# Operands of the second token pair split in place, block order of the last first-layer units, and a later start of the second-layer weight conversion

## The chip, the cores and the metric

The kernel runs on one core of a Trainium2 chip, as one launch. The metric is the device time of one execution in microseconds (us); lower is better. The time before is 1125.38 us, the median of three runs (1124.12 to 1126.78).

## What is computed

```python
def reference(q, k, v, tau, moe_*, moe2_*):
    qn, kn = q / (norm(q, axis=1) + 1e-6), k / (norm(k, axis=1) + 1e-6)   # over 6016 tokens
    a = softmax(kn.T @ qn / tau)                                         # 256 x 256
    x = v @ a                                                            # 6016 x 256
    x = (silu(x @ w_gate) * (x @ w_val)) @ w_out                         # d_ff 1536
    h = x @ w_in                                                         # d_ff 2048
    return (h * clip(h + 3, 0, 6) / 6) @ w_out2
```

All weights arrive as 64-bit floats and are rebuilt on the chip into 32-bit ones. Every product is made of 32-bit values split into a high and a low half (high by a ScalarE copy into the reduced format, low by a VectorE subtraction), and three matmuls: high x high, low x high, high x low.

## The kernel before

The 6016 tokens are cut into six pairs of token blocks: five of 2 x 512 tokens and one of 2 x 448. Channel attention comes first; its 256 x 256 matrix is then folded into the two input weights of the first network (`fold`, L601), so that the first network works on v itself.

**The first pair** (token blocks 0 and 1 of pair 0) is done plainly, while the folded weights are still being made: 24 units `(f, b)` of the loop at L926, f over 12 tiles of hidden channels and b over the two blocks. A unit is 12 matmuls into two PSUM banks, SiLU on ScalarE (L951), a product on VectorE (L952), the split of the result (`plain_split`, L918), and a lagging `back()` (L841) of 6 matmuls with `wo`. Banks go round by `next_bank` (b0, b1, a, d); folds take one, units two.

**All later pairs** use a Strassen-like scheme of seven products (`Cube`, L683): a cube handles one tile i of channels (two for the second network) and both blocks of a pair with products p1 to p7, each of three matmuls, into banks a, b0 or b1, and d. p1 writes bank a, p5 bank d, p6 and p4 and p7 a b bank. Layer 1 has 12 cubes for each of pairs 1 to 5, numbered c = 0 to 59 in the loop at L983; layer 2 follows. A cube also issues two `back()`s of an earlier cube.

**Operands.** For a pair, `prep(u)` (L329) takes the raw tokens, forms the differences that the scheme needs and splits seven operands j = 0 to 6. In the kernel before, most are split into a staging place, stored to DRAM (`opd`, L349), and loaded again into one of nine places op0 to op8 (`load_op`, L398) when the pair before has left it. Pair u's operand j lives in op((7u+j) mod 9). For pair 1 operands 0, 1 and 4 are split directly into their places; 2, 3, 5 and 6 go by DRAM, and `arrive` (L907) issues their four loads in the last two units (L972). The nine steps s1 to s9 of `prep(1)` are put on `todo` at unit 18 and issued by `work(3)` from unit 19 on (L956). During the first pair the op places also hold v (`v_hi`, L472: op0, op3 for block 0, op1, op4 for block 1), and work space of the folds (`FA`: op7, op2; `FS`: op8, op5, L598).

**Second-layer weights.** 16 jobs are rebuilt and split by `convert()` (L252) on VectorE, ScalarE and GpSimd, stored to DRAM (L209, L213, L217) and loaded from there when layer 2 nears (`next_weights`, L878). One call of `convert` advances a clock by one; a job has six steps and a new job starts every three, so the whole takes 51 calls and its pattern repeats every six. In steps of that pattern counted from 0: at 2 one store (L209) and a raw load, at 4 and 1 most ScalarE work, at 5 two stores (L213, and L217, which waits for further ScalarE and GpSimd work) and a raw load (L109). It is called in units 19 to 23 and once per cube from c = 0 (L1023), so call number c + 5 falls in cube c.

**Queues.** Every DMA is issued by SP, in program order, and SP waits there for what the DMA needs. The schedule is written by hand: the order of issue in the program is the order on each engine. At the end of a pair, `back()` copies the finished block from PSUM into tile `xo` (L865) and stores it (`x_d`, L869). `xo` and the raw tokens of the next `prep` (`vr`, L302) share one single buffer, so the load of `vr`, issued in the second cube of a pair, waits for those stores; in the third cube the first step of `prep` on ScalarE (L340) waits for the load.

Of the kernel before, what the change touches and what calls it, by code (L numbers as in the profile page):

```python
# [8 lines left out]
F32 = mybir.dt.float32  # L9
F32R = mybir.dt.float32r  # L10
# [8 lines left out]
def channel_attention_then_two_ffns(  # L19
# [24 lines left out]
    nc = tc.nc  # L44
    P = 128
    NTOK, C = q.shape
    NT = NTOK // P
    CT = C // P
# [128 lines left out]
    def sums(S, a11, a12, a21, a22, engine):  # L177

        engine.tensor_tensor(out=S[:, 0], in0=a21, in1=a22, op=ALU.add)
        engine.tensor_tensor(out=S[:, 1], in0=S[:, 0], in1=a11, op=ALU.subtract)  # L180
        engine.tensor_tensor(out=S[:, 2], in0=a11, in1=a21, op=ALU.subtract)
        engine.tensor_tensor(out=S[:, 3], in0=a12, in1=S[:, 1], op=ALU.subtract)
# [69 lines left out]
    def convert():  # L252

        t = clock[0]
        clock[0] += 1
        for j, steps in enumerate(second):
            if 0 <= t - SPAN * j < len(steps):
                steps[t - SPAN * j]()

    def converted():  # L260
        return clock[0] >= SPAN * (len(second) - 1) + len(second[0])


    passed = [0] * 4

    def load_jobs(ahead=RAW):
        while passed[0] < min(len(jobs), passed[1] + ahead):
            jobs[passed[0]].load()
            passed[0] += 1

# [27 lines left out]
    def op_tile(u, j):  # L298
        ops[u, j] = op_p.tile([P, 2, TB], F32R, tag=f"op{(NQ * u + j) % NS}", name="op")
        return ops[u, j]  # L300
# [19 lines left out]
    def stage(u):  # L320

        i = places_st[0] = places_st[0] + 1
        if u == 0 and i % 3 == 0:
            return op_p.tile([P, 2, TB], F32R, tag="op6", name="sp")
        if 0 < u < NP or u >= NP and i % 4 < 2:
            return op_p.tile([P, 2, TB], F32R, tag=f"op{(NQ * (u + 1) + i % 2) % NS}", name="sp")
        return st_p.tile([P, 2, TB], F32R, tag="st", name="st")

    def prep(u, direct=()):  # L329

        n = pairs[u % NP][1]
        x = load_v(u) if u < NP else load_x2(u - NP)
        b11, b21, b12, b22 = x[:, 0, 0, :n], x[:, 0, 1, :n], x[:, 1, 0, :n], x[:, 1, 1, :n]
        opd[u] = dram.tile([P, NQ, 2, TB], F32, tag=f"opd{u}", name="opd")
        of = {0: b11, 1: b11, 2: b22, 3: b21, 4: b22, 5: b12, 6: b21}
        t = {}

        def hi(j):
            t[j] = op_tile(u, j) if j in direct else stage(u - 1)
            nc.scalar.activation(t[j][:, 0, :n], of[j], AF.Copy)  # L340

        def lo(j):
            nc.vector.tensor_tensor(
                out=t[j][:, 1, :n], in0=of[j], in1=t[j][:, 0, :n].bitcast(F32), op=ALU.subtract
            )
            if j in direct:
                return
            stored.add((u, j))
            nc.sync.dma_start(out=opd[u][:, j, :, :n], in_=t[j][:, :, :n].bitcast(F32))  # L349

        def diff(out, a, b):
            nc.vector.tensor_tensor(out=out, in0=a, in1=b, op=ALU.subtract)

        def s1():
            hi(0)

        def s2():
            hi(4)
            lo(0)
            diff(b11, b12, b11)  # L360

        def s3():
            hi(1)
            lo(4)
            diff(b12, b22, b12)

        def s4():
            hi(5)
            lo(1)
            diff(b22, b22, b11)  # L370

        def s5():
            hi(2)
            lo(5)

        def s6():
            hi(3)
            lo(2)

        def s7():  # L380
            lo(3)
            diff(b21, b21, b22)

        def s8():
            hi(6)

        def s9():
            lo(6)

        return [s1, s2, s3, s4, s5, s6, s7, s8, s9]  # L390

    todo = []

    def work(n):
        for _ in range(min(n, len(todo))):
            todo.pop(0)()
# [8 lines left out]
    with tc.manual_schedule():  # L405

        with tc.tile_pool(name="sm", bufs=1) as sm, tc.tile_pool(name="qk", bufs=AHEAD) as qk_p, tc.tile_pool(
# [63 lines left out]

            def v_hi(b):  # L472
                for k in range(CT):
                    t = v0[b, k] = op_p.tile([P, 2, TB], F32R, tag=f"op{b + 3 * k}", name="v0")
                    nc.scalar.activation(t[:, 0], vraw[:, b, k], AF.Copy)

            def v_lo(b):
# [118 lines left out]
            w_in[1, g] = w1_p.tile([P, 2, 2, NQ, P], F32R, tag=f"w{g}", name="w1")  # L596

        FA = [op_p.tile([P, 2 * CT, CW], F32, tag=f"op{i}", name="FA") for i in (7, 2)]  # L598
        FS = [op_p.tile([P, 2 * CT, CW], F32, tag=f"op{i}", name="FS") for i in (8, 5)]

        def fold(m, g):  # L601

# [37 lines left out]
        def w1_hi(g, o, src):  # L640
            hi = w_in[1, g][:, :, 0, o : o + src.shape[1]]
            nc.scalar.activation(hi, src.rearrange("p o (c f) -> p c o f", c=2), AF.Copy)

        def w1_lo(g, o, src):
            hi, lo = (w_in[1, g][:, :, part, o : o + src.shape[1]] for part in range(2))
            src = src.rearrange("p o (c f) -> p c o f", c=2)
            nc.vector.tensor_tensor(out=lo, in0=src, in1=hi.bitcast(F32), op=ALU.subtract)

        def w1_sums(g):
            fa = FA[g % 2]  # L650
            return lambda: sums(FS[g % 2], fa[:, 0], fa[:, 1], fa[:, 3], fa[:, 2], nc.vector)

        def w1_rest(g):
            fs = FS[g % 2]
            return [lambda: w1_hi(g, S1, fs), lambda: w1_lo(g, S1, fs)]

        turn = [0]

        def next_bank(shape):
            tag = ("b0", "b1", "a", "d")[turn[0] % 4]  # L660
# [216 lines left out]

        def next_weights(g):  # L878

            assert converted()  # L880
            if g < NF2 // CT // 2:
                w_in[2, g] = w1_p.tile([P, 2, 2, NQ, P], F32R, tag=f"w{g}", name="w2i")
                nc.sync.dma_start(out=w_in[2, g].bitcast(F32), in_=wi_d[:, 2 * g : 2 * g + 2])
            else:
                last = g >= NG1
                f0 = (g - NF2 // CT // 2) * per_w2
                nf = min(per_w2, NF2 - f0)
                pool, tag = (const, "wo") if last else (w1_p, f"w{g}")
                t = pool.tile([P, NF1 if last else per_w2, 2, C], F32R, tag=tag, name="w2o")
                w_back[g] = (t, f0, nf)  # L890
                nc.sync.dma_start(out=t[:, :nf].bitcast(F32), in_=w2_d[:, f0 : f0 + nf])
# [19 lines left out]
                load_op(u, j, n)  # L911

        units = [(f, b) for f in range(NF1) for b in range(2)]
        LAG = 3
        n = pairs[0][1]
        h_of, last = None, None
# [9 lines left out]
        for i, (f, b) in enumerate(units):  # L926
            w = w_in[1, f // 2][:, f % 2]
            pss = []
            for row in ((A11, A12), (S1, A22)):
                ps = next_bank([P, TB])  # L930
                for k in range(CT):
                    x = v0[b, k]
                    mm3(
                        ps[:, :n],
                        (w[:, 0, row[k], :], w[:, 1, row[k], :]),
                        (x[:, 0, :n], x[:, 1, :n]),
                        k == 0,
                        k == CT - 1,
                    )
                pss.append(ps)  # L940

            def between():
                pump()
                for go in lows:
                    go()
                lows.clear()

            if h_of:
                plain_split(between)
            h = h_tile(1)  # L950
            nc.scalar.activation(h[:, :n], pss[0][:, :n], AF.Silu)  # L951
            nc.vector.tensor_tensor(out=h[:, :n], in0=h[:, :n], in1=pss[1][:, :n], op=ALU.mult)  # L952
            h_of = (f, b, h)
            if i % 4 == 0 and i:
                todo[:0] = w1_rest(i // 4 - 1)
            work(3 if i > 18 else 1)  # L956
            if i > 18 and passed[3] == NJ1:
                convert()
            if i == 10:
                steps1 = prep(1, (0, 1, 4))  # L960
            g = i // 4 + 1
            if i % 4 in (1, 2) and g < NG1:
                m = i % 4 - 1
                need(m, g)
                for go in lows:
                    go()
                lows = [fold(m, g)]
                if m:
                    todo.append(w1_sums(g))
                    if g == NG1 - 1:  # L970
                        todo.extend(steps1)
            if i >= len(units) - 2:  # L972
                for j in ((2, 5), (3, 6))[i - len(units) + 2]:
                    arrive(1, pairs[1][1], j)
            while len(backs) > LAG - 1:
                back()
        plain_split(lambda: None)
        todo[:0] = w1_rest(NG1 - 1)

        prev = None
        for c, key in enumerate(cubes):  # L983
# [36 lines left out]
            cube.after_p3(prev)  # L1020
            if layer == 2:
                work(i > 1)
            elif not converted():  # L1023
                convert()
            if backs:
                back()
# [46 lines left out]
```

## Time and profile before

| | before |
|---|---|
| median of three runs | 1125.38 us (1124.12 to 1126.78) |
| profiled execution, its own time | 1128.53 us |
| its span | 1126.7 us |
| TensorE busy | 1100.6 us, 98% of the span |
| VectorE, ScalarE, GpSimd busy | 797.7, 765.5, 81.4 us |
| mean granted TensorE clock | 0.992 of full |

The span lies 1.83 us below the time of the same execution; the sums are made in that execution. Matmuls are pipelined, so that the busy time of one (some 385 ns) is longer than the distance from start to start, and lost time is read from the starts. The trace names TensorE PE, its weight loads PEld, VectorE DVE, ScalarE ACT, GpSimd POOL, and the DMA issue of SP SPq.

### The profile page before, as it was taken

The page shows a single profiled execution, that of the slowest core. Times are in us where ns is not written, and L with a number is a line of the kernel's source. Part 1 is how long each engine was busy: PE and PEld are TensorE (multiplying, and loading weights), DVE is VectorE, ACT ScalarE, POOL GpSimd, SP SyncE. Part 2 cuts the span into 40 slices and gives each one's busy share as a digit, 9 for nine tenths or more (in the row PEclk, how much of TensorE's full clock was granted, in tenths as well). Part 3 has the DMA queues.
Part 4 walks back from the last instruction along what each step waited for, and adds up shares of the span by engine and source line. Part 5 has one row for each costly group of instructions (what it writes and reads, how often), then busy time and mean ns, then how long its engine had stood idle before and what let it go on. Part 6 is the DMA issues. An engine that isn't in the chain of part 4 may idle for free.

```text
span 1126.7 us, 13789 instructions
## 1 busy us (share of the span) xinstructions
PE 1100.6 (98%) x4896; PEld 922.0 (82%) x4896; DVE 797.7 (71%) x1254; ACT 765.5 (68%) x1329; POOL 81.4 (7%) x92
## 2 busy tenths in 40 slices
PE   8889998999999999999999999999999999999998
PEld 7768886888788788878899888888888888888897
DVE  6869966687687587677566577677677677676665
ACT  6666755676766676666566677767777777777766
POOL 0000002222131122211000000000000000000000
PEclk9899999999999999999999999999999999999999
DMA  9613405434434623622455722522513413324100
GB/s 336 233 56 94 150 19 182 168 127 165 168 145 141 229 94 138 238 91 113 150 214 220 299 107 98 168 90 99 182 57 124 157 75 136 121 78 134 56 1 33
DMA packets 58053, 154.51 MB, mean 137 GB/s; under 512 B 5248, under 2 KB 18048, under 8 KB 56576
## 3 DMA queue, kind: packets, MB, share of 16 engines
q1 hardware_dynamic: 57984, 153.64, 38.3%
q8 instruction: 38, 0.62, 0.2%
q14 instruction: 31, 0.25, 0.1%
HBM read 91.88 MB, written 61.73 MB: 136 GB/s over the span
## 4 chain that ended last, share of the span: by engine, by line
PE 85%; DMA 7%; DVE 4%; ACT 2%; issue 1%; SPq 0%; DVEq 0%; ACTq 0%
PE o L96 37%; PE ps_b L96 20%; PE ps_a L96 13%; PE ps_d L96 13%; DMA x_d<-xo 2%; DMA vr<-in_vT 1%; DMA op<-opd 1%; DVE acc L535 1%; DMA tk<-in_k 1%; PE ps_b L609 1%; DMA tq<-in_q 1%; DMA raw<-in_moe_w_val 1%; DVE m L131 0%; PE warm L435 0%; DVE h L952 0%
## 5 line engine op out<-in xcount | busy, mean ns | idle before, releaser
L778 DVE TENSOR_TENSOR hl<-h,hl 128x512 fp32r<-128x512 f32 (+1 forms) x312 | 209.9, 685 | 158.9 <-ACT hl L712 152.7
L96 PE MATMUL o<-hl,w2o 128*128 128x512 f32 (+1 forms) x1152 | 287.6, 385 | 0.0
L96 PEld LDWEIGHTS o<-hl,w2o 128*128 128x128 f32 x1152 | 215.9, 188 | 40.8 <-DVE hl L778 0.6
L712 ACT ACTIVATE hl<-h 128x512 fp32r<-128x512 f32 (+1 forms) x312 | 187.7, 617 | 73.3 <-DVE h L762 52.7
L96 PE MATMUL o<-hl,wo 128*128 128x512 f32 (+1 forms) x864 | 218.4, 388 | 3.0 <-DVE wo L159 1.6
L96 PEld LDWEIGHTS o<-hl,wo 128*128 128x128 f32 x864 | 162.3, 188 | 34.7 <-DVE wo L159 2.0
L96 PE MATMUL ps_b<-op,w 128*128 128x512 f32 (+1 forms) x540 | 140.0, 385 | 4.7 <-ACT h L712 3.9
L96 PEld LDWEIGHTS ps_b<-op,w 128*128 128x128 f32 x540 | 101.0, 188 | 25.0 <-ACT h L712 5.6
L716 DVE TENSOR_TENSOR h<-h,ps_d 128x512 f32<-128x512 f32 (+1 forms) x108 | 72.5, 671 | 62.5 <-PE ps_d L96 45.7
L96 PE MATMUL ps_b<-op,w2i 128*128 128x512 f32 (+1 forms) x432 | 112.0, 385 | 0.0
L96 PE MATMUL ps_a<-op,w 128*128 128x512 f32 (+1 forms) x360 | 100.3, 387 | 2.5 <-DMA op<-opd 1.5
L96 PE MATMUL ps_d<-op,w 128*128 128x512 f32 (+1 forms) x360 | 100.1, 387 | 1.4 <-DVE h L952 1.4
L712 ACT ACTIVATE h<-ps_b 128x512 f32<-128x512 f32 (+1 forms) x108 | 63.3, 586 | 53.4 <-PE ps_b L96 52.1
L712 ACT ACTIVATE ps_b<-ps_a 128x512 f32<-128x512 f32 (+1 forms) x108 | 61.9, 573 | 51.4 <-PE ps_a L96 51.2
L96 PEld LDWEIGHTS ps_b<-op,w2i 128*128 128x128 f32 x432 | 81.1, 188 | 15.1
L756 ACT ACTIVATE h<-h,three 128x512 f32<-128x512 f32 (+1 forms) x96 | 68.8, 716 | 34.1 <-DVE h L716 32.5
L716 DVE TENSOR_TENSOR h<-h,ps_b 128x512 f32<-128x512 f32 (+1 forms) x108 | 72.4, 671 | 13.1 <-PE ps_b L96 11.8
L96 PEld LDWEIGHTS ps_a<-op,w 128*128 128x128 f32 x360 | 67.8, 189 | 15.6 <-DMA op<-opd 2.0
L96 PE MATMUL ps_d<-op,w2i 128*128 128x512 f32 (+1 forms) x288 | 79.8, 385 | 0.2 <-DMA op<-opd 0.2
L96 PE MATMUL ps_a<-op,w2i 128*128 128x512 f32 (+1 forms) x288 | 79.8, 385 | 0.0
L96 PEld LDWEIGHTS ps_d<-op,w 128*128 128x128 f32 x360 | 67.9, 189 | 14.3 <-DVE h L952 1.9
L762 DVE SCALAR_TENSOR_TENSOR h<-h 128x512 f32<-128x512 f32 (+1 forms) x96 | 65.0, 677 | 12.5 <-ACT h L756 12.5
(132 smaller groups left out, 1320.8 us busy)
## 6 DMA issues: line engine op xcount, KB each, us to landing
op<-opd SPq DMA_DIRECT2D x60, 512.0 KB, 5.1
opd<-sp SPq DMA_DIRECT2D x44, 512.0 KB, 2.7
opd<-st SPq DMA_DIRECT2D x16, 512.0 KB, 2.6
raw<-in_moe_w_out SPq DMA_DIRECT2D x14, 512.0 KB, 4.2
w2i<-wi_d SPq DMA_DIRECT2D x4, 1792.0 KB, 8.1
op<-opd SPq DMA_DIRECT2D x14, 448.0 KB, 4.1
vr<-in_vT SPq DMA_DIRECT2D x10, 512.0 KB, 4.7
x_d<-xo SPq DMA_DIRECT2D x20, 256.0 KB, 5.3
```

The lines of the kernel that those rows point to most:

```text
L96: nc.tensor.matmul(out, lhsT=w, rhs=x, start=first, stop=last, skip_group_check=True)
L535: nc.vector.tensor_tensor(out=acc[:, :n], in0=acc[:, :n], in1=sq[:, :n], op=ALU.add)
L609: nc.tensor.matmul(ps[:, c, :], lhsT=et[:, d, c * P : (c + 1) * P], rhs=w[:, d, :], start=c == 0 and d == 0, stop=d == CT - 1, skip_group_ ...
L712: nc.scalar.activation(out[:, : self.n], src[:, : self.n], AF.Copy)
L716: nc.vector.tensor_tensor(out=out[:, :n], in0=a[:, :n], in1=b[:, :n], op=ALU.add)
L756: nc.scalar.activation(r[:, : self.n], x[:, : self.n], AF.Relu, bias=three)
L762: nc.vector.scalar_tensor_tensor(out=r[:, :n], in0=r[:, :n], scalar=6.0, in1=x[:, :n], op0=ALU.min, op1=ALU.mult)
L778: nc.vector.tensor_tensor(out=hl[:, 1, :n], in0=h[:, :n], in1=hl[:, 0, :n].bitcast(F32), op=ALU.subtract)
```

## The change

The second pair's seven operands are all split directly into their op places: `prep(1)` has six steps d1 to d6 of its own, and the four stores and four loads are gone. For that, block 1 of v moves to op5 and op6, `FS` for odd groups to op1 and for the last group into a raw-weight buffer, and the last four units go block by block: (10,0), (11,0), (10,1), (11,1). `next_bank` starts two banks later. The second-layer jobs are loaded only from cube c = 1, and `convert` is called from cube c = 3 on instead of from unit 19, so call number c - 3 falls in cube c. `next_weights` asserts only the jobs it needs.

```diff
--- before.py
+++ after.py
@@ -257,14 +257,15 @@
             if 0 <= t - SPAN * j < len(steps):
                 steps[t - SPAN * j]()
 
-    def converted():
-        return clock[0] >= SPAN * (len(second) - 1) + len(second[0])
+    def converted(j=-1):
+        return clock[0] >= SPAN * (j % len(second)) + len(second[0])
 
 
     passed = [0] * 4
+    limit = [NJ1]
 
     def load_jobs(ahead=RAW):
-        while passed[0] < min(len(jobs), passed[1] + ahead):
+        while passed[0] < min(limit[0], passed[1] + ahead):
             jobs[passed[0]].load()
             passed[0] += 1
 
@@ -320,13 +321,11 @@
     def stage(u):
 
         i = places_st[0] = places_st[0] + 1
-        if u == 0 and i % 3 == 0:
-            return op_p.tile([P, 2, TB], F32R, tag="op6", name="sp")
         if 0 < u < NP or u >= NP and i % 4 < 2:
             return op_p.tile([P, 2, TB], F32R, tag=f"op{(NQ * (u + 1) + i % 2) % NS}", name="sp")
         return st_p.tile([P, 2, TB], F32R, tag="st", name="st")
 
-    def prep(u, direct=()):
+    def prep(u):
 
         n = pairs[u % NP][1]
         x = load_v(u) if u < NP else load_x2(u - NP)
@@ -336,14 +335,14 @@
         t = {}
 
         def hi(j):
-            t[j] = op_tile(u, j) if j in direct else stage(u - 1)
+            t[j] = op_tile(u, j) if u == 1 else stage(u - 1)
             nc.scalar.activation(t[j][:, 0, :n], of[j], AF.Copy)
 
         def lo(j):
             nc.vector.tensor_tensor(
                 out=t[j][:, 1, :n], in0=of[j], in1=t[j][:, 0, :n].bitcast(F32), op=ALU.subtract
             )
-            if j in direct:
+            if u == 1:
                 return
             stored.add((u, j))
             nc.sync.dma_start(out=opd[u][:, j, :, :n], in_=t[j][:, :, :n].bitcast(F32))
@@ -387,6 +386,39 @@
         def s9():
             lo(6)
 
+        if u == 1:
+
+            def d1():
+                hi(0)
+                hi(3)
+                lo(0)
+
+            def d2():
+                hi(4)
+                lo(3)
+                diff(b11, b12, b11)
+
+            def d3():
+                lo(4)
+                diff(b12, b22, b12)
+                diff(b22, b22, b11)
+
+            def d4():
+                hi(1)
+                diff(b21, b21, b22)
+                lo(1)
+
+            def d5():
+                hi(6)
+                lo(6)
+
+            def d6():
+                hi(2)
+                hi(5)
+                lo(2)
+                lo(5)
+
+            return [d1, d2, d3, d4, d5, d6]
         return [s1, s2, s3, s4, s5, s6, s7, s8, s9]
 
     todo = []
@@ -471,7 +503,7 @@
 
             def v_hi(b):
                 for k in range(CT):
-                    t = v0[b, k] = op_p.tile([P, 2, TB], F32R, tag=f"op{b + 3 * k}", name="v0")
+                    t = v0[b, k] = op_p.tile([P, 2, TB], F32R, tag=f"op{(3 * k, 5 + k)[b]}", name="v0")
                     nc.scalar.activation(t[:, 0], vraw[:, b, k], AF.Copy)
 
             def v_lo(b):
@@ -596,7 +628,7 @@
             w_in[1, g] = w1_p.tile([P, 2, 2, NQ, P], F32R, tag=f"w{g}", name="w1")
 
         FA = [op_p.tile([P, 2 * CT, CW], F32, tag=f"op{i}", name="FA") for i in (7, 2)]
-        FS = [op_p.tile([P, 2 * CT, CW], F32, tag=f"op{i}", name="FS") for i in (8, 5)]
+        FS = [op_p.tile([P, 2 * CT, CW], F32, tag=f"op{i}", name="FS") for i in (8, 1)]
 
         def fold(m, g):
 
@@ -647,14 +679,21 @@
             nc.vector.tensor_tensor(out=lo, in0=src, in1=hi.bitcast(F32), op=ALU.subtract)
 
         def w1_sums(g):
-            fa = FA[g % 2]
-            return lambda: sums(FS[g % 2], fa[:, 0], fa[:, 1], fa[:, 3], fa[:, 2], nc.vector)
+            def go():
+                fa = FA[g % 2]
+                if g == NG1 - 1:
+                    FS.append(raw_p.tile([P, 2 * CT, CW], F32, tag="raw", name="FS"))
+                sums(fs(g), fa[:, 0], fa[:, 1], fa[:, 3], fa[:, 2], nc.vector)
+
+            return go
+
+        def fs(g):
+            return FS[-1] if g == NG1 - 1 else FS[g % 2]
 
         def w1_rest(g):
-            fs = FS[g % 2]
-            return [lambda: w1_hi(g, S1, fs), lambda: w1_lo(g, S1, fs)]
-
-        turn = [0]
+            return [lambda: w1_hi(g, S1, fs(g)), lambda: w1_lo(g, S1, fs(g))]
+
+        turn = [2]
 
         def next_bank(shape):
             tag = ("b0", "b1", "a", "d")[turn[0] % 4]
@@ -877,14 +916,15 @@
 
         def next_weights(g):
 
-            assert converted()
             if g < NF2 // CT // 2:
+                assert converted(2 * (2 * g + 1))
                 w_in[2, g] = w1_p.tile([P, 2, 2, NQ, P], F32R, tag=f"w{g}", name="w2i")
                 nc.sync.dma_start(out=w_in[2, g].bitcast(F32), in_=wi_d[:, 2 * g : 2 * g + 2])
             else:
                 last = g >= NG1
                 f0 = (g - NF2 // CT // 2) * per_w2
                 nf = min(per_w2, NF2 - f0)
+                assert converted(2 * ((f0 + nf - 1) // CT) + 1)
                 pool, tag = (const, "wo") if last else (w1_p, f"w{g}")
                 t = pool.tile([P, NF1 if last else per_w2, 2, C], F32R, tag=tag, name="w2o")
                 w_back[g] = (t, f0, nf)
@@ -911,6 +951,8 @@
                 load_op(u, j, n)
 
         units = [(f, b) for f in range(NF1) for b in range(2)]
+
+        units[-4:] = [(f, b) for b in range(2) for f in range(NF1 - 2, NF1)]
         LAG = 3
         n = pairs[0][1]
         h_of, last = None, None
@@ -953,11 +995,9 @@
             h_of = (f, b, h)
             if i % 4 == 0 and i:
                 todo[:0] = w1_rest(i // 4 - 1)
-            work(3 if i > 18 else 1)
-            if i > 18 and passed[3] == NJ1:
-                convert()
+            work({18: 2, 19: 2, 20: 3, 21: 2}.get(i, 1))
             if i == 10:
-                steps1 = prep(1, (0, 1, 4))
+                steps1 = prep(1)
             g = i // 4 + 1
             if i % 4 in (1, 2) and g < NG1:
                 m = i % 4 - 1
@@ -969,14 +1009,10 @@
                     todo.append(w1_sums(g))
                     if g == NG1 - 1:
                         todo.extend(steps1)
-            if i >= len(units) - 2:
-                for j in ((2, 5), (3, 6))[i - len(units) + 2]:
-                    arrive(1, pairs[1][1], j)
             while len(backs) > LAG - 1:
                 back()
         plain_split(lambda: None)
         todo[:0] = w1_rest(NG1 - 1)
-
 
 
         prev = None
@@ -1020,7 +1056,10 @@
             cube.after_p3(prev)
             if layer == 2:
                 work(i > 1)
-            elif not converted():
+            elif c == 1:
+                limit[0] = len(jobs)
+                load_jobs()
+            elif c > 2 and not converted():
                 convert()
             if backs:
                 back()
```

## Rows read from the trace of the kernel before

**Rows 1.** The page's first part: busy us (share of the span) and instructions.

```profile
PE 1100.6 (98%) x4896; PEld 922.0 (82%) x4896; DVE 797.7 (71%) x1254; ACT 765.5 (68%) x1329; POOL 81.4 (7%) x92
```

**Rows 2.** Windows: stretch, its us, busy us per engine, granted clock, DMA share, GB/s.

```profile
165.00:183.60 18.60, 18.60 (x83) 15.21 (x82) 15.75 (x26) 9.70 (x18) 3.50 (x4) 1.00 0.23 82
...
183.63:201.71 18.08, 13.39 (x49) 9.94 (x49) 8.93 (x13) 11.36 (x22) 5.20 (x6) 0.91 0.66 230
...
224.00:284.00 60.00, 60.00 (x267) 49.67 (x266) 44.84 (x70) 41.29 (x74) 13.75 (x16) 1.00 0.44 159
```

**Rows 3.** Timeline, PE, first seam: start us, us, instruction, [idle before <-releaser].

```profile
180.91 1.52 PE L96 MATMUL ps_d<-v,w 128*128 128x512 f32 x6
182.27 1.52 PE L96 MATMUL o<-hl,wo 128*128 128x512 f32 x6
184.72 0.96 PE L96 MATMUL ps_a<-op,w 128*128 128x512 f32 x3 [0.93 <-ACT h L951]
187.12 0.97 PE L96 MATMUL ps_d<-op,w 128*128 128x512 f32 x3 [1.43 <-DVE h L952]
...
190.26 0.94 PE L96 MATMUL ps_b<-op,w 128*128 128x512 f32 x3 [0.81 <-DMA op<-opd]
192.72 1.65 PE L96 MATMUL ps_a<-op,w 128*128 128x512 f32 x3 [1.52 <-DMA op<-opd]
...
201.71 0.84 PE L96 MATMUL ps_a<-op,w 128*128 128x512 f32 x3
```

**Rows 4.** Timeline, SP's queue, first seam.

```profile
185.09 2.92 SPq L400 DMA_DIRECT2D op<-opd  x4
```

**Rows 5.** Timeline, PE, the four later seams inside layer 1.

```profile
212.62 0.97 PE L96 MATMUL ps_b<-op,w 128*128 128x512 f32 x3 [0.54 <-ACT h L712]
...
301.17 1.52 PE L96 MATMUL o<-hl,wo 128*128 128x512 f32 x6
303.41 0.97 PE L96 MATMUL ps_b<-op,w 128*128 128x512 f32 x3 [0.72 <-ACT h L712]
...
304.91 0.84 PE L96 MATMUL ps_d<-op,w 128*128 128x512 f32 x3
...
394.77 0.98 PE L96 MATMUL ps_b<-op,w 128*128 128x512 f32 x3 [1.30 <-ACT h L712]
...
486.20 0.96 PE L96 MATMUL ps_b<-op,w 128*128 128x512 f32 x3 [1.34 <-ACT h L712]
```

**Rows 6.** Timeline, ACT, the first prep step at two of these seams.

```profile
302.25 0.63 ACT L340 ACTIVATE sp<-vr 128x512 fp32r<-128x512 f32 x1 [3.78 <-DMA vr<-in_vT]
...
485.09 0.58 ACT L340 ACTIVATE sp<-vr 128x448 fp32r<-128x448 f32 x1 [4.45 <-DMA vr<-in_vT]
```

**Rows 7.** Timeline, SP's queue, a seam with conversion and one after its end.

```profile
289.76 0.37 SPq L217 DMA_DIRECT2D wi_d<-st  x1
290.22 0.42 SPq L109 DMA_DIRECT2D raw<-in_moe_w_out  x1
290.74 2.89 SPq L869 DMA_DIRECT2D x_d<-xo  x4
298.31 0.90 SPq L307 DMA_DIRECT2D vr<-in_vT  x2
...
561.45 3.87 SPq L869 DMA_DIRECT2D x_d<-xo  x4
567.34 0.32 SPq L315 DMA_DIRECT2D x2r<-x_d  x1
```

**Rows 8.** Groups of instructions, shapes apart, 160 to 184 us: xcount | busy, mean ns.

```profile
L343 DVE TENSOR_TENSOR op<-vr,op 128x512 fp32r<-128x512 f32 x3 | 2.1, 686 | 0.0
...
L340 ACT ACTIVATE op<-vr 128x512 fp32r<-128x512 f32 x3 | 1.9, 629 | 4.3 <-issue 2.5 <-DVE w L647 1.7
```

**Rows 9.** Timeline, POOL and DVE at the same moment.

```profile
185.05 1.73 POOL L191 TENSOR_TENSOR st<-m,st 128x256 fp32r<-128x256 f32 x2 [0.95 <-ACT st L202]
...
185.25 1.22 DVE L923 TENSOR_TENSOR hl<-h,hl 128x512 fp32r<-128x512 f32 x1
```

## The prediction, made before the change was run

> **What bounds the kernel now.** I read the page's engine shares first: TensorE (PE) is busy 98% of the span [rows 1], so only places where PE stops, or runs at the lower clock, can give time back. Next the windows. In 224 to 284 us PE is busy 60.00 of 60 us with `convert` running beside it; up to the end of the first pair it is also unbroken, 18.60 of 18.60 us, though VectorE is busy 15.75 us of it. Between them lies the first seam, 183.63 to 201.71 us: PE busy 13.39 of 18.08 us, mean granted clock 0.91, the DMAs at 0.66 [rows 2]. The timeline of PE shows what to see there: four stops, two behind ScalarE and VectorE, which are late with the last unit's banks, and two behind the operands' loads [rows 3]. SP's queue shows that those four loads are issued at 185.09 us [rows 4], after the last unit. Last, the later seams in layer 1: four smaller stops, of which ScalarE is named as the releaser [rows 5], while ScalarE itself had waited for the raw tokens [rows 6].
>
> **The price of the first seam.** Six matmuls take 1.36 us from start to start (180.91 to 182.27 us), or 0.2267 us each, so the last `back()` of the first pair ends at 183.63 us. From there to 201.71 us stand 48 matmuls by the program: 30 of cube 0 (six products of three, as p4 comes a cube later, and two `back()`s of six) and 18 of cube 1 (p1, p5, one `back()`, p4 of cube 0 and p6). At 0.2267 us they take 10.88 us; they take 18.08. **7.20 us are lost**, of which 4.69 us are the four stops (0.93 + 1.43 + 0.81 + 1.52) [rows 3]; the other 2.51 us are matmuls at the lower clock and the restarts.
>
> **What the change does to it.** Four stores, four loads and the two waits for them go: stops three and four. The waits on the last unit's banks go by the shift of `next_bank`: folds and units take 60 banks, so the last unit used a and d, which cube 0's p1 and p5 want first; two banks on, the last unit has b0 and b1 and p1 finds bank a free since the unit before. Cube 0's copy into b0 comes behind that unit's SiLU on the same engine. That removes stops one and two. With no stop there is no fall of the clock.
>
> The splits themselves are not new: seven ScalarE copies of 0.63 us and eleven VectorE subtractions of 0.69 us [rows 8], 4.4 and 7.6 us. Do they still lie beside matmuls? Units 19 to 23 last 5 x 18 x 0.2267 = 20.4 us. VectorE has in them 7.6 us of splits, ten instructions of the units' own (6.9 us), and the last group's sums and three weight halves, which I estimate at 3.6 us from about five times 0.69. That makes 18.1 us, without the conversion that is taken away there: 2.3 us of room. Only d6 is in the last unit; its operand 2 is wanted by p6, 12 matmuls or 2.7 us after 183.63, and it needs two subtractions (1.4 us) behind the last unit's product. I cost the splits at nothing; the cover gone, they would cost as in the third rival. Places are free when the steps come: op1 and op8 after the sums' halves of groups 3 and 4, op2 after the last sums, op0 and op3 after unit 21, which the new order puts two units ahead of d6; op4 is used by nobody. The last sums' raw buffer is free because all first-layer jobs are past reading theirs by unit 19 (that was the condition under which `convert` ran there). Gain: 0 at the least if the splits are late by what the loads cost, 7.20 at most; I take 7.20.
>
> **The later seams.** At the seam near 303 us the 12 matmuls from 301.17 to 304.91 us should take 2.72 us and take 3.74: 1.02 lost, 0.30 above the 0.72 shown as idle. With the same 0.30 added to the other three (0.54, 1.30, 1.34) [rows 5] the four lose 0.84 + 1.02 + 1.60 + 1.64 = 5.10 us. ScalarE waited 3.78 us in the second of them and 4.45 us in the last [rows 6]; 3.78 of waiting cost PE 1.02, so about 2.76 us of wait are covered. Why are the tokens late? Their load needs the buffer that the last stores of `xo` read. SP issues those stores until 293.63 us, right behind a weight store and a raw load (289.76, 290.22), and the token load follows at 298.31: 4.68 us later. At the seam of the last pair no conversion runs any more: stores until 565.32, load at 567.34, 2.02 us later [rows 7]. So the conversion's transfers cost the seam 2.66 us. In the changed kernel the pattern of `convert` moves by eight cubes: at a seam's first cube it stood at step 5 (two stores and a raw load) and then stands at 9 mod 6 = 3, which issues no DMA, and the next cube at 4, none either; step 5 comes with the third cube, behind the token load. The waits become 3.78 - 2.66 = 1.12 and 1.79 us, under the covered 2.76, so **5.10 us go**. In the first of these seams the stores are earlier too, as block 0 ends one `back()` sooner, and the first two raw loads come behind the token load. What is late next: nothing that I see up to layer 2. Bounds: 0, if the stores land no sooner, and 5.10.
>
> **Moved work.** All 51 calls stay, with every store and load; they end in cube 53 instead of 45. The first weight load of layer 2 needs early jobs alone, the last job is done well before its load. In cubes a call costs PE nothing (60.00 of 60 us [rows 2]), so I cost the eight later calls at nothing, covered by the last pair's slack. ScalarE work of steps 4 and 1 now falls in a seam's second cube: four activations by the code, at about the 0.63 of [rows 8] an estimate of 2.5 us; it is under the covered 2.76 us, beside a shorter wait, but this is where the seams could be lost again. At the start the first fold uses bank a, from which ScalarE must first copy; its second matmul wanted that copy anyway. Between nothing and a stop like the first in [rows 3], 0.93 us; nearest is nothing, I take 0.1.
>
> **Sum.** 7.20 + 5.10 - 0.10 = 12.2 us. The profiled execution took 1128.53 us and would take 1116.3; it lies 3.15 us above the median of the runs, so from the median, 1125.38 - 12.2 = **1113.2 us**.
>
> **Rivals.** *The first seam alone.* The tokens are late for reasons of their own, or the moved ScalarE work takes the wait's place; for it speaks that ScalarE's slack at a seam is 2.76 us and it gets some 2.5 us more, against it the unbroken seam of the last pair. 1125.38 - 7.2 = 1118.2 us.
>
> *The waits on engines stay.* Stops one and two persist because ScalarE and VectorE are still behind with d5, d6 and the last unit, and the clock falls all the same: of the first seam only the load stops are saved, 0.81 + 1.52 = 2.33 us, with the seams 7.43: 1118.0 us. For it: VectorE's room is only 2.3 us; against it: the shifted banks.
>
> *Slower: the split burst overruns VectorE.* Place: units 19 to 23. A VectorE instruction took 1.22 us instead of 0.69 while GpSimd worked [rows 9]. At 1.22 us the 18.1 us become 32.0, 11.6 more than the units cover, and with the lower clock's 2.51 the seam costs 14.1 instead of 7.20; less the seams' 5.10 the kernel is 1.8 us slower, 1127.2. It decides from about 1.15 us per instruction. Against it: GpSimd has nothing to do there any more. The Trainium skill, "SBUF — State Buffer", section "SBUF: two separate sides", has a rule for such pairs: a GpSimd operation and a VectorE operation with two SBUF inputs take one port pair for a whole instruction, and "the other fully blocks". The 1.22 us agree with it; by that rule the removal of the conversion speaks against this rival.
>
> *The change does nothing*: what the seams lose comes back further on, at another full engine; PE's unbroken stretches speak against that. 1125.4 us.
>
> **How the numbers follow.** Forecast 0.62 (1113.2), first seam alone 0.18 (1118.2), engine waits stay 0.10 (1118.0), nothing 0.04, slower 0.06. Faster by more than 0.2%, about what a measurement here can tell from no change, is 0.90, within it 0.04, slower 0.06. The range runs from the fastest run shown less all gains, 1124.12 - 12.3 = 1111.8, to 1119.2, a microsecond above the two rivals at 1118; it holds some 0.85, from which I leave a little for what no row shows.
>
> **What would show it.** Right: no loads of `op` from `opd` near the first seam, p1 of cube 0 directly behind the `back()`, granted clock 1.00 there, ScalarE's wait for the tokens under 2.8 us at each seam, and no PE stop behind it. Wrong: a PE stop at p6 of cube 0 behind a VectorE subtraction (operand 2 late); ScalarE late at a seam's third cube with its conversion work ahead of it; a stop at the start of layer 2 behind a weight load.

## The result, and the profile after

The changed kernel takes 1115.74 us (median of four runs, 1115.18 to 1118.32), the kernel before 1125.60 us beside it (1124.12 to 1126.78): 9.86 us less, a ratio of 0.9914 with a 95% interval of 0.9898 to 0.9929. That is faster, inside the range of 1111.8 to 1119.2, and 2.5 us above the forecast of 1113.2. The profiled execution took 1115.36 us, 13.17 us under the profiled one of before. The page of the changed kernel, its engine shares:

```profile
PE 1094.3 (98%) x4896; PEld 919.5 (83%) x4896; DVE 794.9 (71%) x1254; ACT 768.2 (69%) x1329; POOL 78.3 (7%) x92
```

Against [rows 1] the shares hardly move, because the span falls by 13.1 us and PE's busy time with it, by 6.3: the lost time was in part idle and in part matmuls that took longer, such as the 2.51 us of the prediction at the first seam (busy 13.39 us before, 10.88 after). The share hides both. The first seam of the changed kernel on PE, from the last unit on (start us, us, instruction):

```profile
181.85 1.52 PE L96 MATMUL o<-hl,wo 128*128 128x512 f32 x6
183.21 0.84 PE L96 MATMUL ps_a<-op,w 128*128 128x512 f32 x3
183.89 0.84 PE L96 MATMUL ps_d<-op,w 128*128 128x512 f32 x3
184.57 1.52 PE L96 MATMUL o<-hl,wo 128*128 128x512 f32 x6
185.93 0.84 PE L96 MATMUL ps_b<-op,w 128*128 128x512 f32 x3
186.61 0.84 PE L96 MATMUL ps_a<-op,w 128*128 128x512 f32 x3
...
194.09 0.84 PE L96 MATMUL ps_a<-op,w 128*128 128x512 f32 x3
```

None of these lines has the bracket that marks an idle time; the four of [rows 3] are gone. From 183.21 to 194.09 us are 10.88 us, just what 48 matmuls take at 0.2267. The same stretch as a window (columns as in [rows 2]) has PE busy throughout and a clock of 1.00 instead of 0.91:

```profile
183.21:194.09 10.88, 10.88 (x50) 9.01 (x48) 4.84 (x8) 7.65 (x14) 0.00 (x0) 1.00 0.14 50
```

SP's queue of the changed kernel at the seam near 286 us, which answers to [rows 7]:

```profile
279.87 3.96 SPq L908 DMA_DIRECT2D x_d<-xo  x4
285.94 0.90 SPq L308 DMA_DIRECT2D vr<-in_vT  x2
288.42 0.37 SPq L213 DMA_DIRECT2D wi_d<-st  x1
296.23 0.37 SPq L217 DMA_DIRECT2D wi_d<-st  x1
296.65 0.46 SPq L109 DMA_DIRECT2D raw<-in_moe_w_out  x1
```

The token load is issued 2.11 us after the last block store (283.83), not 4.68, and step 5's stores and raw load stand behind it. ScalarE's wait for tokens, 3.78 us at this seam before [rows 6], does not appear there any more. Two such waits are left, one right after the first seam and one at the last pair's seam, where the tokens of layer 2 are loaded (total us, times, longest):

```profile
ACT sp L339 <- DMA vr<-in_vT: 0.5, 1, 0.5
```

```profile
ACT sp L339 <- DMA x2r<-x_d: 1.4, 1, 1.4
```

Both are covered: from its first `back()`, near 85 us, to the seam into layer 2, near 630 us, PE stops nowhere.

### The profile page after: what moved, and what is told of

It is laid out like the page before. It is cut to its first block, busy times and chain, and to the rows that moved or that the text cites. A ratio compares the mean times of both kernels' runs of the same rounds, so it can differ in the third digit from the quotient of the medians.

```text
span 1113.6 us, 13768 instructions
## 1 busy us (share of the span) xinstructions
PE 1094.3 (98%) x4896; PEld 919.5 (83%) x4896; DVE 794.9 (71%) x1254; ACT 768.2 (69%) x1329; POOL 78.3 (7%) x92
## 4 chain that ended last, share of the span: by engine, by line
PE 92%; DVE 3%; DMA 2%; issue 1%; ACT 1%; SPq 0%; DVEq 0%; ACTq 0%
PE o L96 40%; PE ps_b L96 22%; PE ps_a L96 14%; PE ps_d L96 14%; DVE acc L567 1%; DMA tk<-in_k 1%; PE ps_b L641 1%; DMA tq<-in_q 1%; DMA raw<-in_moe_w_val 1%; DVE m L131 0%; PE warm L467 0%; PE ps_a L641 0%; PE ps_d L641 0%; DVE m L120 0%; DVE m L137 0%
## 5 line engine op out<-in xcount | busy, mean ns | idle before, releaser
L96 PEld LDWEIGHTS ps_a<-op,w 128*128 128x128 f32 x360 | 67.6, 188 | 12.3
L96 PEld LDWEIGHTS ps_d<-op,w 128*128 128x128 f32 x360 | 67.6, 188 | 12.3
```

What stands on the lines that cost most here:

```text
L96: nc.tensor.matmul(out, lhsT=w, rhs=x, start=first, stop=last, skip_group_check=True)
```

## The experiments

**How steady are the stops?** The kernel before, unchanged, profiled a second time.

> The kernel before, unchanged, profiled a second time. Theory A (the profiled execution of before lost more than its others): this execution takes about 1125.5 us, some 3 us under the first profiled one, and its trace shows where: the waits of the four later seams or of the first one are shorter by 2 to 3 us in sum. Theory B (the seams cost the same each time): the seams lose the same 7.2 and 5.1 us, within 0.5, and the 3 us lie elsewhere, ahead of the first unit.

Measured: ratio 0.9999 (0.9989 to 1.001), the profiled execution 1122.93 us, 5.6 us under the first one. PE at its first seam, and at two later ones:

```profile
183.27 0.96 PE L96 MATMUL ps_a<-op,w 128*128 128x512 f32 x3 [0.93 <-ACT h L951]
185.67 1.35 PE L96 MATMUL ps_d<-op,w 128*128 128x512 f32 x3 [1.44 <-DVE h L952]
186.81 2.77 PE L96 MATMUL o<-hl,wo 128*128 128x512 f32 x6
189.37 0.91 PE L96 MATMUL ps_b<-op,w 128*128 128x512 f32 x3
190.88 0.96 PE L96 MATMUL ps_a<-op,w 128*128 128x512 f32 x3 [0.60 <-DMA op<-opd]
...
198.48 0.84 PE L96 MATMUL ps_a<-op,w 128*128 128x512 f32 x3
```

```profile
299.33 0.96 PE L96 MATMUL ps_b<-op,w 128*128 128x512 f32 x3 [0.47 <-ACT h L712]
...
480.84 0.96 PE L96 MATMUL ps_b<-op,w 128*128 128x512 f32 x3 [1.36 <-ACT h L712]
```

Stops one and two are as in [rows 3]; three and four, which wait for DMAs, are 0.60 instead of 2.33 us. From the end of the last `back()` (180.81 + 1.36 = 182.17) to 198.48 us are 16.31 us, so 5.43 us are lost, not 7.20. The loads themselves were not much quicker: the product behind the last of them (190.88 here, 192.72 in [rows 3]) starts 8.71 us after the last `back()`, against 9.09. That is 0.38 of the 1.77 us. The other 1.39 lie behind that product, and there the clock differs. Windows of the first trace (behind the last load) and of the second (ahead of it):

```profile
192.72:196.95 4.23, 4.23 (x12) 3.42 (x13) 1.20 (x2) 1.07 (x2) 0.00 (x0) 0.64 0.34 130
```

```profile
185.67:189.37 3.70, 3.70 (x9) 2.92 (x10) 1.24 (x2) 2.64 (x4) 0.00 (x0) 0.55 1.01 347
```

After its stops PE ran for some us largely at the lower of its two clock levels (1.2 instead of 2.4 GHz) in both. In the first trace that stretch came after the last load, where it delays everything behind it; in the second it came while the loads were still on their way, so that PE was slow instead of idle, and behind the last load the granted clock was 1.00. So the idle marks 2.33 and 0.60 overstate how much the loads differ.

Start to start, the four later seams lose 0.26, 0.76, 0.34 and 1.65 us, 3.01 in sum, not 5.10. Here it is the tokens: SP issues their load 3.91, 4.52, 4.21 and 5.80 us after the last block store, against 4.66, 4.68, 5.29 and 5.63 in the first trace. Theory A holds in that the lost time at the seams varies from execution to execution. A further 1.3 us lie ahead of the first fold (it starts at 58.67 us, against 59.97), so theory B's place has a share too.

**The conversion alone.** The kernel before with the later conversion; the asserts and the limit on loads as in the change.

```diff
-            if i > 18 and passed[3] == NJ1:
-                convert()
...
-            elif not converted():
+            elif c == 1:
+                limit[0] = len(jobs)
+                load_jobs()
+            elif c > 2 and not converted():
                 convert()
```

> The kernel before with the later conversion alone; operands, places, order and banks as before. If the parts add as the prediction has them: the later seams gain 5.1 us (no stop at them), the first seam still loses most of its 7.2 us, so some 5 to 6 us below before. Rival (ScalarE and VectorE are late in the last units because of the conversion in them): stops one and two go as well, and the first seam loses only 2 to 4 us.

Measured: 1118.54 us beside 1125.35, ratio 0.994 (0.9921 to 0.9959), or 6.8 us less. PE at its first seam:

```profile
182.08 0.84 PE L96 MATMUL ps_a<-op,w 128*128 128x512 f32 x3
182.76 0.84 PE L96 MATMUL ps_d<-op,w 128*128 128x512 f32 x3
183.44 1.52 PE L96 MATMUL o<-hl,wo 128*128 128x512 f32 x6
185.83 0.92 PE L96 MATMUL ps_b<-op,w 128*128 128x512 f32 x3 [0.87 <-DMA op<-opd]
188.29 0.98 PE L96 MATMUL ps_a<-op,w 128*128 128x512 f32 x3 [1.54 <-DMA op<-opd]
```

The rival was right as to the first two stops: with the old banks they are gone, so the conversion in the last units had made ScalarE and VectorE late. The loads still stop PE for 2.41 us, and there is no stop at the later seams of layer 1. The first seam still loses 4.57 us here (182.08 to 197.53, less 10.88), a size between the two expectations; most of what the stops leave open is again a stretch at a mean granted clock of 0.60 behind the last load (188.29 to 192.50).

**The operands alone.** The changed kernel with the conversion where it was; the last sums stand in a staging buffer, since the raw ones are then in use.

```diff
-    limit = [NJ1]
+    limit = [len(jobs)]
...
-                    FS.append(raw_p.tile([P, 2 * CT, CW], F32, tag="raw", name="FS"))
+                    FS.append(st_p.tile([P, 2 * CT, CW], F32, tag="st", name="FS"))
...
+            if i > 18 and passed[3] == NJ1:
+                convert()
...
-            work(1)
+            work(1 if c else 2)
...
-            elif c == 1:
-                limit[0] = len(jobs)
-                load_jobs()
-            elif c > 2 and not converted():
+            elif not converted():
```

> The operands in place, the new order and banks, but the conversion as before, from unit 19 on and with step 5 at the seams (the last sums stand in a staging buffer, and both of their weight halves come in cube 0). Prediction's view: the first seam is whole in spite of the conversion, the later seams lose as before, some 4 to 7 us below before. Rival (the conversion in the last units makes ScalarE and VectorE late, and with them d6): p6 of cube 0 or a product behind it stops by 1 to 3 us, and little of the first seam's gain is left.

Measured: 1118.42 us beside 1125.43, ratio 0.994 (0.9926 to 0.9955), 7.0 us less. The first seam is whole, as the prediction's view had it. But VectorE shows how near it came; there, GpSimd beside it, and the PE line that needs the result:

```profile
184.13 1.92 DVE L342 TENSOR_TENSOR op<-vr,op 128x512 fp32r<-128x512 f32 x2
```

```profile
183.89 1.60 POOL L191 TENSOR_TENSOR st<-m,st 128x256 fp32r<-128x256 f32 x2
```

```profile
186.58 0.84 PE L96 MATMUL ps_b<-op,w 128*128 128x512 f32 x3
```

The last two subtractions end at 186.05 us, 0.5 us ahead of p6, and take 1.92 us together while GpSimd works; in the changed kernel they end at 184.00, 1.9 us ahead of p6, and take 1.28:

```profile
182.72 1.28 DVE L342 TENSOR_TENSOR op<-vr,op 128x512 fp32r<-128x512 f32 x2
```

The later seams stop again, in this execution at two of them, 0.56 and 0.84 us; start to start the later seams lose 2.41 us (360.77 us from the first p1 to the last pair's first product, against 358.36 in the changed kernel).

**The banks.** The changed kernel with the old banks, and the kernel before with the new ones, each by this line or its reverse:

```diff
-        turn = [2]
+        turn = [0]
```

> The changed kernel with the banks not shifted: the last unit uses a and d again. Prediction's step: stops one and two at p1 and p5 come back, 1 to 2.4 us, no fall of the clock. Rival (they came from the conversion in the last units, ScalarE and VectorE being late): under 1.0 us in all, since the last unit's SiLU and product are ready sooner.

Measured: 1115.07 us, ratio to before 0.9904 (0.9884 to 0.9925), no stop at the first seam. The shift is worth nothing once the conversion is out of the last units.

> The kernel before with the banks shifted alone. Prediction's step taken alone: stops one and two go (2.4 us), the loads then stop PE sooner and longer. If the loads set the end of the seam, the time stays within 0.5 us of before; if the engines did, it falls by 2 us.

Measured: 1126.94 us beside 1125.43, ratio 1.0012 (1.0003 to 1.0021): some 1.5 us slower. Its PE:

```profile
183.32 0.84 PE L96 MATMUL ps_a<-op,w 128*128 128x512 f32 x3
184.00 0.84 PE L96 MATMUL ps_d<-op,w 128*128 128x512 f32 x3
184.68 1.52 PE L96 MATMUL o<-hl,wo 128*128 128x512 f32 x6
189.76 0.94 PE L96 MATMUL ps_b<-op,w 128*128 128x512 f32 x3 [3.56 <-DMA op<-opd]
192.20 1.65 PE L96 MATMUL ps_a<-op,w 128*128 128x512 f32 x3 [1.50 <-DMA op<-opd]
...
194.92 2.76 PE L96 MATMUL o<-hl,wo 128*128 128x512 f32 x6
```

Stops one and two do go (0.93 and 1.43), but PE then arrives sooner at a load that lands when it did, and stop three grows from 0.81 to 3.56 us. Part of the first seam's loss belonged to two causes at once, and taking one away gave nothing. It was even slower than either expectation, and the trace shows where: behind the last load PE runs at the lower clock (granted 0.50 from 192.20 to 196.50), and the seam loses 8.15 us (183.32 to 202.35, less 10.88), more than either trace of before. The runs agree: nine of its ten have a mean granted clock of at most 0.992, against one of the thirteen of before beside them.

**The order of the units.** The changed kernel without its line for the last four units; and with the old banks too.

```diff
-        units[-4:] = [(f, b) for b in range(2) for f in range(NF1 - 2, NF1)]
```

> The changed kernel with the last four units in the old order, so that op0 and op3 are left after the last unit but one instead of two units sooner. If the room in the last unit decides: d6 waits for that unit's matmuls and p6 stops by 0.5 to 2 us. Rival (d6 has room anyway, its copies come after that unit's matmuls in either order): no difference, under 0.3 us.

> The changed kernel with both the old banks and the old order of the last units. If these two steps are worth nothing: within 0.7 us of the changed kernel and no stop at the first seam. If each covers for the other: a stop of 1 us or more at p1, p5 or p6 of cube 0.

Measured: 1116.22 us (ratio 0.9917, 0.99 to 0.9935) and 1116.07 us (0.9927, 0.9909 to 0.9945), and no stop at either's first seam. Order and banks are worth nothing measurable, alone or together.

**The seams of the conversion's pattern.** Three variants of the changed kernel move the cube in which the conversion begins, and so what it does at a seam: to 7 (step 5 at the seam), to 4 (step 2), and to 7 with each raw load held back by two cubes. Their edits, in this order:

```diff
-            elif c > 2 and not converted():
+            elif c > 6 and not converted():
...
-            elif c > 2 and not converted():
+            elif c > 3 and not converted():
...
             passed[1] += 1
-            load_jobs()
...
-            elif c > 2 and not converted():
+            elif c > 6 and not converted():
                 convert()
+                if c % 3 == 2:
+                    load_jobs()
```

> The changed kernel with conversion begun in cube 7 instead of 3, so that its pattern stands at the seams as it stood before: step 5 (two weight stores, a raw load) in cubes 12, 24, 36, 48. Theory (the transfers and the wait of step 5 ahead of the block stores make the tokens late): the first seam stays whole, the seams at cubes 12, 24 and 36 lose some 1.0, 1.6 and 1.6 us again, the one at 48 perhaps as much; 4 to 6 us above the changed kernel. Rival (the seams gained from something else, such as fewer transfers in the first pair): no stop returns, under 0.5 us.

> Conversion begun in cube 4: step 2 stands at a seam, one weight store and one raw load ahead of the block stores, but nothing that SP waits for as long as in step 5. Theory 1 (the transfers ahead are what is late): half or more of step 5's loss, 2 to 4 us. Theory 2 (SP's wait for step 5's second store is what is late): no loss, under 0.5 us.

> As the kernel with step 5 at the seam, but each raw load is issued two cubes later, at the end of a seam's third cube, so none lies ahead of the block stores; the two weight stores and SP's wait stay. Theory 1 (the transfers ahead): the tokens come 1 to 2 us sooner than with step 5 at the seam and half or more of its loss goes. Theory 2 (SP's wait): the loss stays within 0.5 us of that kernel's.

Measured beside 1124.6 us for the kernel before: 1122.96 (ratio 0.9983, 0.9973 to 0.9993), 1116.39 (0.9927, 0.9912 to 0.9942) and 1117.74 us (0.994, 0.9925 to 0.9955). Step 5 at the seams costs 7.2 us against the changed kernel's 1115.74 (7.8 by the two ratios to before); the other two cost 0.7 and 2.0 (1.5 and 2.9 by the ratios), and their intervals overlap the changed kernel's, so that these two costs are not clear of the noise. SP's queue at the seam of cube 12, first with step 5 there:

```profile
281.51 0.37 SPq L217 DMA_DIRECT2D wi_d<-st  x1
281.98 0.42 SPq L109 DMA_DIRECT2D raw<-in_moe_w_out  x1
282.49 2.92 SPq L908 DMA_DIRECT2D x_d<-xo  x4
289.71 0.90 SPq L308 DMA_DIRECT2D vr<-in_vT  x2
```

then with step 2 there:

```profile
279.87 0.38 SPq L109 DMA_DIRECT2D raw<-in_moe_w_in  x1
280.34 3.47 SPq L908 DMA_DIRECT2D x_d<-xo  x4
287.02 0.90 SPq L308 DMA_DIRECT2D vr<-in_vT  x2
```

and with step 5 but the raw load later:

```profile
279.66 0.36 SPq L217 DMA_DIRECT2D wi_d<-st  x1
280.12 2.67 SPq L907 DMA_DIRECT2D x_d<-xo  x4
285.36 0.90 SPq L307 DMA_DIRECT2D vr<-in_vT  x2
```

From the last block store's issue to the token load's the three take 4.30, 3.21 and 2.57 us, the changed kernel 2.11. So at this seam a raw load ahead costs about 1.1 us, the weight store about 0.5, both together 2.2; at the next two it is 0.6 to 1.0, 0.5 to 0.6 and 2.0 to 3.0. That SP is held adds its own share: counted from cube 0's p1, the token load comes 3.53 us later with step 5 than in the changed kernel, and 1.34 of these are that the last block store is itself issued later. ScalarE's waits there are 3.2, 1.0 and 0.7 us, and only the first stops PE (by 0.15 us in this execution). Each theory was half right: the transfers cost more than SP's wait, as theory 1 had it for the third variant, but neither a raw load nor a store alone uses up the cover at cube 12.

At cubes 12, 24 and 36 step 5 brings back 2.2 us of loss (0.45, 0.82 and 0.95 from start to start), where before lost 4.26 in its first trace and 2.75 in its second: the mechanism is shown, the whole size is not. Most of the variant's cost lies at a seam where before converted nothing any more, the last pair's, cube 48. With step 5 ScalarE waits 6.0 us there and PE stops for 3.34, with the raw load later 4.6 and 2.00; the last pair's 80.83 us of the changed kernel become 86.92 and 83.69. The layer-2 weight load is issued right behind the token load there, but the token load lands 4.8 us after its issue, as against 4.7 in the changed kernel. What is late is its issue: 17.58 and 16.26 us after the pair's first p1, against 13.56. The stop on PE with the raw load later, in cubes that are shorter by their 448 columns:

```profile
562.15 0.87 PE L96 MATMUL ps_b<-op,w 128*128 128x448 f32 x3 [2.00 <-ACT h L750]
```

**The changed kernel again.**

> The changed kernel again, on the chip of the next three. Theory A (it was the kernel before whose stops vary from execution to execution): the changed kernel has no stop at the seams to vary, its trace shows none again, 1115 to 1117 us. Theory B (both vary alike): a stop of 0.5 us or more at a seam.

Measured: 1115.98 us beside 1125.43, ratio 0.9923 (0.9908 to 0.9938). No stop at the seams of layer 1, and a wait of ScalarE for tokens of at most 1.6 us. Theory A holds. No variant is measurably faster than the changed kernel.

## Why the prediction was right, and where its size was off

- **First seam, 7.20 us:** the changed kernel loses 0.00 us there, in both of its traces. The term was right for the execution that it was read from, and 1.77 us too large for the second one, where the low clock fell ahead of the last load instead of behind it (1.39 of the 1.77).
- **Later seams, 5.10 us:** all gone, by the mechanism named: step 5 behind the token load, the load 2.11 us after the stores (forecast 2.02). Again the size is one execution's; the second lost 3.01.
- **The step that was off** is "from the median, 1125.38 - 12.2". It took losses from an execution that the text itself put 3.15 us above the median, and subtracted them whole from the median. Against its own execution the sum gave 1116.3 and 1115.36 was measured. With the second trace's terms it is 5.43 + 3.01 = 8.4 us; the measured 9.86 lies between 8.4 and 12.3. Of the 5.6 us between the two traces of before, 1.77 lie at the first seam, some 2.1 at the later ones and 1.3 ahead of the first fold.
- **Causes inside the first seam:** the prediction gave stops one and two to the shift of the banks. The runs show two cures, each enough for these two stops: the shift (banks alone, conversion left in) or the later conversion (old banks), and in the changed kernel the shift is not needed. The other 2.51 us, matmuls at the lower clock, went with the stops, as forecast: the granted clock is 1.00 there.
- **The splits cost nothing:** right, and the new order of the units, which the prediction counted on for op0 and op3, was not needed for it.
- **Cover at a seam, about 2.76 us:** right, and nearly a constant. In both traces of before, ScalarE's wait less PE's loss from start to start is 2.76 to 2.82 us at all four later seams (in the second: 3.02, 3.53, 3.10 and 4.47 of wait, 0.26, 0.76, 0.34 and 1.65 of loss). The prediction took it from one seam. The idle mark alone would mislead: waits of 3.0 and 3.1 us left none. The waits that it forecast for the changed kernel, 1.12 and 1.79 us, were too long: at most 0.2 us is left at cubes 12, 24 and 36, in both of its traces.
- **Moved work and start, 0 and 0.1 us:** no stop in the last pair; the first fold in bank a waited 0.47 us instead of 0.23, so 0.24 us.
- **The rivals:** the slower one fell: VectorE's seven split subtractions take 0.68 to 0.69 us each here. With GpSimd at work the last two took 1.92 us, which agrees in kind with the Trainium skill, "SBUF — State Buffer", section "SBUF: two separate sides"; even then the seam held, by 0.5 us. *The first seam alone* and *the waits on engines stay* fell too, as no stop is left at either place. The parts do not add: 6.8 us for the conversion alone and 7.0 for the operands alone, but 9.5 to 9.9 together, because each takes part of the other's term: the first leaves 4.57 us of the first seam's 7.20, the second 2.41 of the later seams' 5.10.

## What to carry to other kernels

Before a gap from one profiled execution is subtracted from a median, profile the kernel a second time: stops behind late engine work repeated to 0.01 us here, the later seams lost 5.10 us once and 3.01 once. And read the loss from the starts, not from the idle marks: 2.33 and 0.60 us of idle marks stood behind loads that released PE at times only 0.38 us apart, since a low clock can fall ahead of a load, where it is hidden, or behind it, where it is not. Where an engine and a load are late at the same place, curing one only moves the wait (0.93 and 1.43 us went, and the stop at the load grew by 2.75); price them as one stop. In a queue that issues in order, the place of a periodic job against the other period is worth checking by itself: begun in cube 7 instead of cube 3, the same 51 calls cost 7.2 us more.

## What was not expected

The clock in the first units is also one execution's. In most traces it fell in 84 to 92 us, after PE's waits for `wo`; with the conversion alone it did not, and that execution came to its first cube 122.07 us after the first fold, against 123.66 before (to the end of the last `back()`, 183.63). The windows of the two, that one first:

```profile
84.00:92.00 8.00, 6.73 (x30) 5.55 (x30) 7.90 (x16) 4.07 (x7) 0.00 (x0) 1.00 0.22 68
```

```profile
84.00:92.00 8.00, 6.80 (x23) 5.40 (x24) 7.90 (x16) 4.06 (x7) 0.00 (x0) 0.79 0.22 68
```

The busy times are alike, the granted clock is 1.00 or a mean of 0.79, and 30 or 23 matmuls were done. What decides between them the runs do not show.
